# Attention and MLP on one core: the second batch's coarse head pairs go between its local groups, their E into unit 0's h buffers

## The chip, the cores and the metric

The kernel runs on 1 core of one Trainium2 chip. The metric is the time of one execution on the device in microseconds, median of 3 runs. Lower is better. Engines are called PE (TensorE), DVE (VectorE), ACT (ScalarE), POOL (GpSimd) and SP (SyncE, which here only issues DMAs).

## What is computed

Four batches of 576 positions and 512 features (8 heads of 64). Attention is the sum of two parts: a coarse one, on q, k and v averaged over groups of four positions (144 x 144 scores a head), and a local one, in which a position sees only its neighbours at a distance under 4. Then a Fourier mix with a residual, a normalisation, an MLP with a residual, and a gated output layer.

```python
q_d, k_d, v_d = (x.reshape(B, H, Sd, 4, D).mean(axis=3) for x in (q, k, v))
out = np.repeat(sm_attn(q_d, k_d, v_d), 4, axis=2) + local_attn(q, k, v)   # |i - j| < 4
x = out.transpose(0, 2, 1, 3).reshape(B, S, H * D)
u = x + np.real(np.fft.fft(np.fft.fft(x, axis=1), axis=2))
un = (u - u.mean(-1)) / np.sqrt(var + 1e-06)
x = u + np.maximum(un @ w_ch1, 0.0) @ w_ch2
gate = 1.0 / (1.0 + np.exp(-causal_conv5(x, conv_w)))
out = (gate * (x @ w_val)) @ w_out
```

All in float32; large products run as three float16 products (high by high, low by high, high by low).

## The kernel before

**Units.** The MLP runs over 12 units of 192 positions, three to a batch, numbered 0 to 11; unit 3 is the first of the second batch (b = 1). A unit is 8 groups of hidden features (`h_group`, L1116, tile `ph`) and 8 of the second product (`c_group`, L1132, tile `pc`); it needs its normalised input `uh`, `ul` from `ln` (L986 to L1051). Unit 0 alone runs in float32 (`steps32`, L1072): its hidden features lie in four `h32` tiles, three of them from the "acc" tag with three buffers (L1079), read by its `c_group` (L1098), two groups a tile. `moe2_steps` (L1166) is the output layer of a unit: taps of the convolution, `val` (L1235), `out` (L1251).

**The order of the work.** Every piece of work is a Python step with a weight. `put` and `spread` (L1345 to L1353) give each step a position on one axis, where n to n + 1 is unit n; before 0 lies the start (first batch, weights of the MLP). All steps are then called in order of position (L1408). From the instructions so recorded, with that order as priority, the framework's planner makes the fixed order of each engine's queue, by its own estimate of durations: an instruction of lower priority goes ahead where the other isn't ready or finds no buffer. `urgent` (L174) raises a step's priority by a number of instructions; the Fourier steps ("F") and `ln` ("N") are raised by 3000, the second batch's local and coarse steps aren't.

**Attention of a batch** (`attn_steps`, L423). `dense` (L487) is the local part, in three groups of windows: `scores(g)` (L522: matmuls into two banks `dS`, maximum, exponentials `dP`, sums, products) and `values(g)` (L580: transposes `dPT`, copies `PT`, matmuls `dO`, copies to X). `lowres` (L696) is the coarse part: a step for `base`, the squares of v for a scale (L680), and for each of four head pairs a step with score matmuls `sc` (L713), maxima `nm` (L720), exponentials `E` (L727) and their normalisation (POOL for b = 1, L736), and a step with transposes `eT` (L753), copies `ET`, matmuls `po` with the pooled v (L763) and the copy to `base` (L767). Then `base` is added to X (L786), the second half of X goes through DRAM to be mirrored (L795 to L802, L862), and the Fourier steps follow (L836 to L965).

**Positions of the second batch.** The local part, the four loads and sums of v (`pool_v4`, L643) and the sums of k stand in `P_D[1]` = 0.02 to 0.94; the coarse part and all that follows in `P_E[1]` = 0.96 to 1.85; `ln` of unit 3 at `P_L[1]` = 2.1.

**Buffers.** The tag "E" (three buffers) holds E, ET, PT, `ptv` (the partial sum of v) and later the Fourier tiles. `dS` and `sc`, with the Fourier sums, take turns on the two PSUM banks of tag "t"; `dPT`, `dO`, `eT`, `po`, `val` and `out` on the two of tag "s" (L35 to L39). v's pieces use the two buffers of "pr". The weights of the output layer come as `raw` tiles into the "k" and "v" buffers of the local v windows (L339).

**Loads.** All go through `load` (L183) on SP's queue. While `chain["on"]` holds (up to position `S_CH` = 0.9, L1364) each is ordered behind the one loaded before it; from then on the planner puts them in any order. SP issues in order: one that waits for its buffer holds the rest.

Of the kernel before, what the change touches and what calls it, by code (L numbers as in the profile page):

```python
# [9 lines left out]
F32 = mybir.dt.float32  # L10
# [3 lines left out]
AF = mybir.ActivationFunctionType  # L14
# [5 lines left out]
SD = S // 4  # L20
QC = SD // 2
# [20 lines left out]
NORM_V = ((1, 0), (1, 1))  # L42
LN_V = ((0, 0), (0, 2), (1, 0), (2, 0), (3, 0))
CHAIN = True
S_CH = 0.9
S_LD = (-12.14, -11.9)
S_L1 = -11.85
S_K = -11.75
# [12 lines left out]
N_WARM = (8, 5, 14, 2, 2, 2)  # L61
S_G1 = (-6.8, -6.7)
S_G2 = (0.2, 0.44)
P_D = {1: (0.02, 0.94), 2: (2.0, 3.2), 3: (4.4, 6.0)}
P_E = {1: (0.96, 1.85), 2: (3.3, 4.5), 3: (6.1, 7.4)}
P_L = {1: 2.1, 2: 4.9, 3: 8.5}
P_T0 = ((0.75, 0.93), (1.0, 1.3), (1.6, 2.0))
EN_G = (1,)
SUM_V = ()
# [59 lines left out]
def attn_moe_kernel(ctx, tc, q_t, k_t, v_t, w1, w2, w_val, conv_t, w_out, c_feat, c_seq, c_band, c_eye, out):  # L129
# [48 lines left out]
        else:  # L178
            f()

    chain = {"on": CHAIN, "last": None}

    def load(**kw):  # L183

        if chain["on"] and chain["last"] is not None:
            with tc.issue_after(chain["last"]):
                i = nc.sync.dma_start(**kw)
        else:
            i = nc.sync.dma_start(**kw)
        chain["last"] = i.ins  # L190
# [232 lines left out]
    def attn_steps(b):  # L423
# [63 lines left out]
        def dense(sp):  # L487
# [170 lines left out]
            if b == 0:  # L658
# [3 lines left out]
                lr = pools[2:] + [(0.1, lambda kc=kc: pooled_v0(vw, kc)) for kc in range(3)] + steps[:]  # L662
                steps[:] = low
            es = [{} for _ in GROUPS]
            if first:
                steps.extend([(1.3, lambda: scores(0, es[0])), (2.6, lambda: scores(1, es[1]))] + pools + lr[2:4])
                steps.extend([(2.6, lambda: scores(2, es[2])), lr.pop(4)] + lr[4:7])
                del lr[:7]
            for r in range(len(GROUPS) + 1):
                if r < len(GROUPS) and not first:  # L670
                    steps.append((1.3 * len(GROUPS[r]), lambda r=r: scores(r, es[r])))
                if r > 0:
                    steps.append((0.5 * len(GROUPS[r - 1]), lambda r=r: values(r - 1, es[r - 1])))
                if r > LR0:
                    for _ in range(5):
                        if lr:
                            steps.append(lr.pop(0))
            steps.extend(lr + v1)

            def squares():  # L680
                for g in range(len(GROUPS)):
                    A.activation(out=vw[g], in_=vw[g], func=AF.Square, accum_out=d["ssv"][:, g:g + 1])

            if not first:
                d["squares"] = squares


        def scale_x():
# [7 lines left out]
        def lowres():  # L696
# [6 lines left out]
            for a in range(H // 2):  # L703
                lr = {}

                def f(a=a, lr=lr):
# [3 lines left out]
                    for qc in range(2):  # L710
                        for par in range(2):
                            r = slice(par * 64, par * 64 + 64)
                            T.matmul(  # L713
                                out=pss[par][:, qc], lhsT=d["qkT"][r, 0, a, qc * QC:(qc + 1) * QC],
                                rhs=d["qkT"][r, 1, a, :], start=True, stop=True,
                            )
                    for par in range(2):
                        ps = pss[par]
                        nm = tiny.tile([QC, 2], F32, tag="nm", name="nm")
                        i = V.tensor_reduce(out=nm, in_=ps, axis=AX.X, op=ALU.max)  # L720
                        if b == 0:
                            gates.append(i.ins)
                        A.activation(out=nm, in_=nm, func=AF.Copy, scale=-SCALE / 16)
                        E = prp.tile([QC, 2, SD], F32, tag="E", name="E", bufs=3) if b else startup.tile([QC, 2, SD], F32, tag="E0", name="E0", bufs=4)
                        su = tiny.tile([QC, 2], F32, tag="lsu", name="lsu")
                        for qc in range(2):
                            A.activation(  # L727
                                out=E[:, qc], in_=ps[:, qc], func=AF.Exp, scale=SCALE / 16,
                                bias=nm[:, qc:qc + 1], accum_out=su[:, qc:qc + 1],
                            )  # L730
                        V.tensor_scalar(out=su, in0=su, scalar1=1e-9, scalar2=None, op0=ALU.add)
                        i = V.reciprocal(out=su, in_=su)
                        if b == 0 and a == H // 2 - 1 and par:
                            gates1.append(i.ins)
                        if b in EN_G:
                            mul(G, E, E, su.unsqueeze(2).to_broadcast([QC, 2, SD]))  # L736
                        else:
                            for qc in range(2):
                                A.activation(out=E[:, qc], in_=E[:, qc], func=AF.Copy, scale=su[:, qc:qc + 1])
                        lr[par] = E  # L740
# [35 lines left out]
        else:  # L776
            dense(None)
            d.setdefault("cuts", []).append(len(steps))
            lowres()
            n_chain = len(steps)  # L780

        @step(2.7)
# [562 lines left out]
    def put(pos, f):  # L1345
        events.append((pos, len(events), f))
# [14 lines left out]
    spread([(1.0, lambda i=i: sumsq_w(i, "w2", i == 8, i == 15)) for i in range(8, 16)], *S_G2)  # L1361
    put(S_G2[1], lambda: urgent(w2_scale, "S"))
    put(S_LW2, lambda: [load_w(i) for i in range(8, 11)])
    put(S_CH, lambda: chain.update(on=False))  # L1364
    for steps, p in ((st[0]["loads"], S_LD), (a0[:c0], S_T0), (a0[c0:c1], S_S0), (a0[c1:], S_F0)):
        spread(steps, *p)
    for r, f, p in ((W1_ORDER, w_in, S_W1), (W1_ORDER[:4], w_out_, S_C0), (W1_ORDER[4:], w_out_, S_C1), (range(8, 16), w_in2, S_W2)):
# [92 lines left out]
```

## Time and profile before

| | us |
|---|---|
| median of 3 runs (733.96 to 735.82) | 734.01 |
| the profiled execution | 733.22 |
| its span, first to last instruction | 731.4 |
| PE busy | 682.0 (93%) |
| DVE busy | 468.5 (64%) |
| ACT busy | 326.3 (45%) |
| POOL busy | 111.7 (15%) |
| mean granted clock of PE | 0.965 of full |

The profiler records one execution. A line is an instruction, or several alike, on one engine: line of the kernel, operation, written tile <- read tiles, shape. Times in a timeline are us from the start of the span. Idle time in brackets is that of the engine just before the instruction, with what ended it. Busy times of pipelined matmuls overlap, so the time of a row of several is not their sum. The granted clock is a share of full speed (1.00 is 2.4 GHz).

### The profile page before, as it was taken

The numbers are of one execution on the slowest core, as the hardware profiler recorded it, in microseconds if no ns is written. First come the engines' busy times: TensorE is split into PE (matmuls) and PEld (weight loads), VectorE is DVE, ScalarE is ACT, GpSimd is POOL, SyncE is SP. The second block draws the span as 40 slices with busy tenths as digits, with TensorE's granted clock in tenths as the row PEclk, the third lists the DMA queues.
The fourth block names the chain that finished last, engine by engine and source line by source line (L and its number), as shares of the span: only waits on it lengthen the run. The fifth ranks groups of instructions, "written<-read, shape, count | busy, mean of one in ns | idle before, by whom it ended". The sixth has DMA issues, their size and how long they took to land. (4 is left out here: it accounts for less than half of the span.)

```text
span 731.4 us, 18333 instructions
## 1 busy us (share of the span) xinstructions
PE 682.0 (93%) x7785; PEld 594.6 (81%) x7785; DVE 468.5 (64%) x983; ACT 326.3 (45%) x998; POOL 111.7 (15%) x158
## 2 busy tenths in 40 slices
PE   8488799997999877999999999999999999999997
PEld 4255598987899666868898898789899989999895
DVE  4888699997856597365976824829635572633324
ACT  2674273894433356756433825644413132222212
POOL 0400012124112121330203106003100010000000
PEclk9758999999999979999999999999999999999999
DMA  9965251524413100240230001003000000000001
GB/s 245 380 222 179 81 213 61 133 74 146 143 50 100 61 2 17 77 141 16 72 109 2 24 17 43 16 2 95 20 16 15 2 15 17 2 15 2 30 2 44
DMA packets 27574, 53.01 MB, mean 72 GB/s; under 512 B 2112, under 2 KB 16320, under 8 KB 26468
## 3 DMA queue, kind: packets, MB, share of 16 engines
q1 hardware_dynamic: 27492, 51.84, 22.1%
q8 instruction: 61, 1.00, 0.6%
q14 instruction: 21, 0.17, 0.1%
HBM read 45.34 MB, written 8.26 MB: 73 GB/s over the span
## 5 line engine op out<-in xcount | busy, mean ns | idle before, releaser
L1123 PE MATMUL ph<-uh,W 128*128 128x192 f16 x1408 | 195.2, 247 | 1.4 <-ACT uh L1049 1.4
L1123 PEld LDWEIGHTS <-W 128*128 128x128 f16 x2112 | 176.6, 98 | 9.2 <-issue 7.2
L1123 PE MATMUL ph<-ul,W 128*128 128x192 f16 x704 | 173.9, 247 | 2.5 <-DVE ul L1050 2.5
L1143 PE MATMUL pc<-hh,W 128*128 128x192 f16 x1232 | 171.4, 246 | 0.0
L1143 PEld LDWEIGHTS <-W 128*128 128x128 f16 x1848 | 152.8, 98 | 8.3 <-issue 7.1
L1143 PE MATMUL pc<-hl,W 128*128 128x192 f16 x616 | 150.9, 246 | 1.2 <-DVE hl L166 1.2
L166 DVE SCALAR_TENSOR_TENSOR hl<-ph,hh 128x384 f16<-128x384 f32 x88 | 48.4, 551 | 93.0 <-ACT hh L1127 92.6
L1127 ACT ACTIVATE hh<-ph 128x384 f16<-128x384 f32 x88 | 43.3, 492 | 102.9 <-PE ph L1123 99.9
L166 DVE SCALAR_TENSOR_TENSOR W<-X,cw,W 128x192 f32<-128x192 f32 x160 | 61.7, 440 | 1.2 <-ACT W L1198 1.0
L1235 PE MATMUL val<-yy,W 128*128 128x192 f16 x576 | 54.8, 251 | 0.0
L1235 PEld LDWEIGHTS <-W 128*128 128x128 f16 x576 | 49.6, 100 | 3.1 <-issue 1.0
L570 ACT ACTIVATE dP<-dS,dmx 128x64 f32<-128x64 f32 x160 | 47.9, 333 | 0.7 <-PE dPT L591 0.3
L1251 PE MATMUL out<-W,gh 128*128 128x512 f16 x144 | 45.6, 379 | 0.0
L570 ACT ACTIVATION_READ_ACCUMULATOR dP<-dS,dmx 128x1 f32 x160 | 36.3, 227 | 0.0
L166 DVE SCALAR_TENSOR_TENSOR W<-W,W 128x1024 int32<-128x1024 int32 x24 | 28.4, 1215 | 0.1
L1251 PE MATMUL out<-W,gl 128*128 128x512 f16 x72 | 27.3, 379 | 0.0
L727 ACT ACTIVATE E<-sc,nm 72x144 f32<-72x144 f32 x64 | 23.5, 376 | 6.7 <-PE po L763 3.7
L1143 PE MATMUL pc<-hh,Wz 128*128 128x192 f16 x176 | 25.1, 246 | 1.1 <-DVE X L172 1.1
L1143 PEld LDWEIGHTS <-Wz 128*128 128x128 f16 x264 | 22.0, 98 | 4.1 <-DVE X L172 1.4
L1251 PEld LDWEIGHTS <-gh 128*128 128x128 f16 x144 | 14.1, 98 | 13.7 <-issue 0.2
L1085 PE MATMUL ph<-u,W 128*128 128x192 f32 x128 | 24.2, 344 | 1.0 <-DVE u L1008 1.0
L1198 ACT ACTIVATE W<-X,cw 128x192 f32<-128x192 f32 x40 | 15.6, 451 | 20.9 <-DVE X L166 19.0
(246 smaller groups left out, 1203.0 us busy)
## 6 DMA issues: line engine op xcount, KB each, us to landing
W<-in_moe_w_ch_dram SPq DMA_DIRECT2D x12, 1024.0 KB
v<-in_v_dram SPq DMA_DIRECT2D x32, 144.0 KB
out_dram<-osb SPq DMA_DIRECT2D x17, 256.0 KB
vw<-in_v_dram SPq DMA_DIRECT2D x16, 256.0 KB
X<-in_q_dram SPq DMA_DIRECT2D x6, 576.0 KB
kT<-in_k_dram SPq DMA_DIRECT2D x4, 582.0 KB
X<-in_moe_w_ch_dram SPq DMA_DIRECT2D x2, 1024.0 KB
raw<-in_moe_w_ch_dram SPq DMA_DIRECT2D x4, 512.0 KB
```

The costliest lines, as they stand in the source:

```text
L166: return eng.scalar_tensor_tensor(out=out, in0=in0, scalar=scalar, in1=in1, op0=op0, op1=op1)
L570: A.activation(out=s_[:, z, a], in_=pss[par][:, z, a], func=AF.Exp, scale=SCALE, bias=mx[:, par, z, a:a + 1], accum_out=su[:, par, z, a:a ...
L727: A.activation(out=E[:, qc], in_=ps[:, qc], func=AF.Exp, scale=SCALE / 16, bias=nm[:, qc:qc + 1], accum_out=su[:, qc:qc + 1],)
L1085: i = T.matmul(out=ps[:, e], lhsT=W[AT[kc * 2 + m // 8] + 1][:, o:o + 128], rhs=u()[:, kc, :], start=(kc == 0), stop=(kc == 3))
L1123: T.matmul(out=ps[:, e], lhsT=w1_ap(pw, kc, 2 * g + e), rhs=uh[px][:, kc, :], start=(t == 0), stop=(t == 11))
L1127: A.activation(out=h_, in_=ps, func=AF.Relu)
L1143: T.matmul(out=ps[m // 2][:, m % 2], lhsT=w2_ap(pw, kk, m), rhs=x[px][:, e, :], start=(kk == 0 and (pw, px) == (0, 0) and m % 2 == 0), sto ...
L1198: A.activation(out=m, in_=x, func=AF.Copy, scale=w)
L1235: T.matmul(out=ps[:, e], lhsT=wv_ap(pw, kc, 2 * mh + e), rhs=m_["y"][px][:, kc, :], start=(t == 0), stop=(t == 11))
L1251: T.matmul(out=ps, lhsT=(gh, gl)[px][:, kc, t * 128:(t + 1) * 128], rhs=wo_ap(pw, kc), start=(n == 0), stop=(n == 11))
```

## The change

- The four head pairs of the second batch no longer stand behind its local part. `dense` itself calls `lowres` for b = 1 and mixes the steps: scores 0, scores 1, values 0, first half of pair 0, scores 2, values 1, second half of pair 0, first half of pair 1, values 2, and the rest of the pairs; the pieces of v stand between them from the start, the sums of k ahead of all.
- E of a pair is one tile [72, 2, 2, 144] of the tag "acc" for b = 1.
- `S_CH` is 1.3, so all of the second batch's loads are in the chain, and every later load is ordered behind the last of the chain.
- `P_D[1]` is 0.02 to 1.2 and holds local and coarse part; `P_E[1]` is 1.21 to 1.75 and holds what follows; `P_L[1]` is 1.9.

```diff
-S_CH = 0.9
+S_CH = 1.3
-P_D = {1: (0.02, 0.94), 2: (2.0, 3.2), 3: (4.4, 6.0)}
-P_E = {1: (0.96, 1.85), 2: (3.3, 4.5), 3: (6.1, 7.4)}
-P_L = {1: 2.1, 2: 4.9, 3: 8.5}
+P_D = {1: (0.02, 1.2), 2: (2.0, 3.2), 3: (4.4, 6.0)}
+P_E = {1: (1.21, 1.75), 2: (3.3, 4.5), 3: (6.1, 7.4)}
+P_L = {1: 1.9, 2: 4.9, 3: 8.5}
@@ load
+        elif chain["after"] is not None:
+            with tc.issue_after(chain["after"]):
+                i = nc.sync.dma_start(**kw)
@@ dense (squares is defined ahead of this)
+            if b == 1:
+                low = steps[:]
+                del steps[:]
+                lowres()
+                lr = steps[:]
+                steps[:] = low + v1[4:] + lr[:1]
+                cs = lr[2:]
+                sx = cs.pop(3)
+                sg = lambda g: (1.3 * len(GROUPS[g]), lambda: scores(g, es[g]))
+                og = lambda g: (0.5 * len(GROUPS[g]), lambda: values(g, es[g]))
+                steps.extend([sg(0), v1[0], sg(1), v1[1], og(0), cs[0], v1[2], sg(2), v1[3], og(1), cs[1], cs[2], og(2),
+                          cs[3], cs[4], (0.1, squares), sx, cs[5], cs[6], cs[7]])
+                return
@@ lowres
+                    Ep = acc_t("E", [QC, 2, 2, SD]) if b == 1 else None
...
-                        E = prp.tile([QC, 2, SD], F32, tag="E", name="E", bufs=3) if b else startup.tile([QC, 2, SD], F32, tag="E0", name="E0", bufs=4)
+                        E = Ep[:, par] if b == 1 else prp.tile([QC, 2, SD], F32, tag="E", name="E", bufs=3) if b else startup.tile([QC, 2, SD], F32, tag="E0", name="E0", bufs=4)
@@ attn_steps
-            lowres()
+            if b > 1:
+                lowres()
@@ the plan
-    put(S_CH, lambda: chain.update(on=False))
+    put(S_CH, lambda: chain.update(on=False, after=chain["last"]))
```

## Rows read from the trace of the kernel before

**Rows 1.** Busy time by stretch: bounds, length, five engines, granted PE clock, DMA.

```profile
90.00:252.00 162.00, 153.41 (x1691) 139.93 (x1691) 130.44 (x234) 86.25 (x244) 35.90 (x50) 0.99 0.36 111
140.00:200.00 60.00, 54.01 (x694) 48.07 (x692) 52.30 (x115) 39.29 (x116) 18.20 (x22) 1.00 0.39 119
252.00:279.60 27.60, 16.16 (x220) 13.65 (x218) 25.96 (x62) 15.24 (x50) 5.52 (x6) 0.80 0.01 2
258.27:268.51 10.24, 7.72 (x65) 6.45 (x66) 9.11 (x24) 7.15 (x26) 2.56 (x2) 0.50 0.01 2
278.75:282.16 3.41, 2.67 (x17) 2.52 (x17) 1.68 (x4) 3.41 (x25) 0.00 (x0) 0.50 0.00 0
```

**Rows 2.** Timeline of PE, 250 to 284: start, us, what, idle before.

```profile
258.85 0.59 PE L254 MATMUL tot<-ss_wo,ones 128*128 128x1 f32 x2 [4.86 <-DVE ss_wo L366]
...
263.51 0.98 PE L1002 MATMUL st<-sq,ones 128*128 128x192 f32 x2 [1.94 <-DVE sq L172]
...
279.49 0.32 PE L1123 MATMUL ph<-ul,W 128*128 128x192 f16 x1 [2.47 <-DVE ul L1050]
```

**Rows 3.** Timeline of DVE, 254 to 281.

```profile
278.49 0.95 DVE L1050 TENSOR_TENSOR ul<-uc,uh 128x768 f16<-128x768 f32 x1
```

**Rows 4.** Timeline of POOL, 138 to 218.

```profile
177.30 0.94 POOL L172 TENSOR_TENSOR vr<-vr,ptv 72x256 f32<-72x256 f32 x1
...
216.34 1.21 POOL L172 TENSOR_TENSOR X<-X,base 128x576 f32<-128x576 f32 x1 [5.47 <-ACT base L767]
```

**Rows 5.** Timeline of PE, 138 to 204: third local group's and coarse scores.

```profile
141.68 0.60 PE L538 MATMUL dS<-bandb 128*128 128x512 bf16 x2
...
154.88 0.89 PE L713 MATMUL sc<-qkT 64*72 64x144 f32 x8
...
171.58 0.71 PE L713 MATMUL sc<-qkT 64*72 64x144 f32 x4
...
190.44 0.89 PE L713 MATMUL sc<-qkT 64*72 64x144 f32 x8
...
198.62 0.71 PE L713 MATMUL sc<-qkT 64*72 64x144 f32 x4
```

**Rows 6.** Timeline of DVE, 138 to 218: maxima of the head pairs.

```profile
159.62 0.81 DVE L720 TENSOR_REDUCE nm<-sc 72x2 f32<-72x288 f32 x2
...
179.65 0.44 DVE L720 TENSOR_REDUCE nm<-sc 72x2 f32<-72x288 f32 x1
...
194.21 0.80 DVE L720 TENSOR_REDUCE nm<-sc 72x2 f32<-72x288 f32 x2
...
200.62 0.44 DVE L720 TENSOR_REDUCE nm<-sc 72x2 f32<-72x288 f32 x1
...
202.38 0.45 DVE L720 TENSOR_REDUCE nm<-sc 72x2 f32<-72x288 f32 x1
```

**Rows 7.** Timeline of ACT, 138 to 218: exponentials of the head pairs.

```profile
172.11 0.36 ACT L727 ACTIVATE E<-sc,nm 72x144 f32<-72x144 f32 x1
...
204.64 0.37 ACT L727 ACTIVATE E<-sc,nm 72x144 f32<-72x144 f32 x1
```

**Rows 8.** Timeline of SP's queue, 120 to 220: DMA issues.

```profile
162.60 0.36 SPq L189 DMA_DIRECT2D raw<-in_moe_w_val_dram  x1
163.06 0.34 SPq L187 DMA_DIRECT2D v<-in_v_dram  x1
```

**Rows 9.** Tile h: its readers; ns least, median, most, first and last start.

```profile
L1098 PE MATMUL pc<-h,W x128: 326/326/430, 118.1 to 154.6; 128*128 128x192 f32 x128
```

**Rows 10.** Third batch: timelines of DVE (405 to 413) and PE (446 to 452).

```profile
411.29 0.95 DVE L1050 TENSOR_TENSOR ul<-uc,uh 128x768 f16<-128x768 f32 x1
...
450.21 0.25 PE L1123 MATMUL ph<-uh,W 128*128 128x192 f16 x1
```

**Rows 11.** Timeline of POOL: the same addition at two places.

```profile
160.35 2.32 POOL L172 TENSOR_TENSOR ptv<-v 72x256 f32<-72x256 f32 x1
...
303.41 0.72 POOL L172 TENSOR_TENSOR ptv<-v 72x256 f32<-72x256 f32 x1
```

More of the change, by code (lines that the diff above doesn't have):

```diff
@@ L179, in urgent @@
             f()
-    chain = {"on": CHAIN, "last": None}
+    chain = {"on": CHAIN, "last": None, "after": None}
     def load(**kw):
@@ L664, in dense, with squares @@
             es = [{} for _ in GROUPS]
+            def squares():
+                for g in range(len(GROUPS)):
+                    A.activation(out=vw[g], in_=vw[g], func=AF.Square, accum_out=d["ssv"][:, g:g + 1])
+            if not first:
+                d["squares"] = squares
             if first:
@@ L678, in dense @@
             steps.extend(lr + v1)
[L680 to L685, printed above, removed]
         def scale_x():
```

## The prediction

> **What bounds the kernel now.** I read the busy time of the engines in a few stretches first, then TensorE's own timeline where it idles, then the chain of work behind that idle time. From 90 to 252 us TensorE is busy 153.4 of 162 us, at full clock; from 252 to 279.6 us it is busy only 16.2 of 27.6 us and the mean granted clock falls to 0.80 [rows 1]. So the kernel is bound by TensorE almost everywhere, and this hole is the largest loss behind the start. It costs 27.6 - 16.16 = 11.4 us of idleness. In two pieces in and just behind it the clock is granted at 0.5 (1.2 GHz, the lower of the two levels): 7.72 and 2.67 us of busy time there would take half as long at 2.4 GHz, so they lose 3.9 + 1.3 = 5.2 us. Together 16.6 us.
>
> The gaps say what the hole waits for. TensorE sits idle 4.86 us before 258.85, 1.94 us before 263.51 and 2.47 us before 279.49 [rows 2]. The last ends when `ul`, the low half of the second batch's first normalised unit, is written at 278.49 + 0.95 = 279.44 us [rows 3]: unit 3 can't begin without it. Ahead of `ul` stand that unit's normalisation and the batch's Fourier part, which began when the last coarse result had been added to X, at 216.34 + 1.21 = 217.55 us [rows 4]. From there to `ul` it takes 279.44 - 217.55 = 61.9 us. Unit 2 ends near 252 us, so the coarse part of the second batch comes about 27 us too late.
>
> Why is it late? The score matmuls of its four head pairs start at 154.88, 171.58, 190.44 and 198.62 us [rows 5]. The maxima of the first are taken at 159.62 us [rows 6], but its last E is written only at 172.11 us [rows 7]. In the first pair exponentials stand 11 us behind their maxima, in the last the first one stands at 204.64 us [rows 7], 3.6 us behind a maximum that ended at 200.62 + 0.44 us [rows 6]. They share three "E" buffers with PT, ET and the pooled v. And v itself is late: the fourth transfer is issued at 163.06 us, right behind a weight transfer at 162.60 that had blocked SP's queue [rows 8], so `vr` is whole only at 177.30 + 0.94 us [rows 4]. No pair can finish before.
>
> **The change, part by part.** *Positions.* From the steps' weights I worked out where each step is placed, in units of the main loop. The third group's scores move from 0.46 to 0.52, the last group's values from 0.79 to 0.90; the first head pair from 0.97 to 0.42, the second from 1.02 to 0.81, the third from 1.08 to 0.99, the fourth from 1.13 to 1.10. The addition to X stays (1.19 to 1.21). The positions alone thus promise nothing for the end; what they change is who gets a buffer first. The narrower range of the Fourier steps and the earlier normalisation cost and bring nothing by my count: those are marked urgent, so they run when their inputs are there.
>
> *E in another buffer.* The four pair tiles take the three buffers that unit 0's h had. The matmuls that read h run from 118.1 to 154.6 us [rows 9], the first buffer's in the first quarter of that, so the first pair finds its buffer free at 142 us, and the fourth takes the first pair's again. This removes the wait for "E".
>
> *The two score banks.* Local scores and head pairs take turns on two PSUM banks. Let H be the time for which a pair holds them. The third group's scores got them at 141.68 us and gave them up at 154.88 us [rows 5], which is 13.2 us. In the new order the first pair goes ahead of that group, the others behind it. So the fourth pair starts at 141.68 + H + 13.2 + 2H = 154.9 + 3H. In before it took 217.55 - 198.62 = 18.9 us from there to X, of which 3.2 us was the wait for "E" (3.6 less 0.4 for scaling the maximum): 15.7 us. So X is ready at **170.6 + 3H**. With the "E" wait taken out H is the time to the end of the second maximum plus 2.6 us (scaling, and four exponentials at 0.57 us): 160.43 - 154.88 + 2.6 = 8.1; 180.09 - 171.58 + 2.6 = 11.1; 195.01 - 190.44 + 2.6 = 7.2; 202.83 - 198.62 + 2.6 = 6.8 [rows 5 to 7]. The mean is 8.3; H lies between 6.8 and 11.1. As it stood in before, with the "E" wait, the first pair held them 172.66 - 154.88 = 17.8 us.
>
> With H = 8.3 X is ready at 195.5 us instead of 217.55, **22 us sooner** (26.5 at 6.8; 13.7 at 11.1).
>
> *v.* The eight transfers stay in the chain, so they go out one after another from 129 us on, ahead of the third batch's X and of the weights for the second layer. SP's queue holds these behind them; each waits for VectorE or GpSimd to free a buffer. `vr` should be whole near 160 us, before the first pair needs it. What is moved behind is covered: the third batch's unit starts at 450.21 us with its `ul` written at 411.29 + 0.95 us [rows 10], 38 us of slack; the weights are first used inside the hole. If that cover goes, each us that these weights come late is a us in which the hole can't be filled, up to the 4 us below. No DMA is added.
>
> *The squares* for the scale of the second batch move from 0.97 to 1.08: three ScalarE operations, still before the Fourier steps. I take nothing; the lower bound is nothing too, the upper about 2 us, the time in which those weights wait for the v buffers that the squares still read.
>
> *Crowding.* From 140 to 200 us VectorE is busy 52.3 of 60 us, ScalarE 39.3, and TensorE idles 6.0 us [rows 1]. The work of the first pairs moves into its first half, where weights are still being split. Nothing in before shows this mixture. I bound it from -2 us (part of the idle time there is the pairs' own and goes) to +6 us (it doubles) and take +2, nearer to the first since only two pairs move by much.
>
> *The sum.* `ul` comes at 279.4 - 22 = 257.4 us. Unit 2's end leaves 5.2 us of hole, in which the 1.1 us of weight squares and perhaps val matmuls fit; I leave 2 us idle (0 to 4). Of 16.6 us, 14.6 is won, less 2 for crowding: 12.6 us. The profiled execution took 733.2 us, of which the span is 731.4; 733.2 - 12.6 = 720.6. The median of the runs is 0.8 us higher, 734.0, so I predict **721 us**. With H = 6.8, no idle rest and -2 for crowding, 18.6 us are won: 715 us.
>
> A rule that speaks against the change stands in the Trainium skill, "SBUF — State Buffer", section "SBUF: two separate sides": a GpSimd instruction and a VectorE one with two SBUF inputs share a port pair as an exclusive lock, and the later one fully blocks; by it the sum comes out at the first rival's time, without it at the forecast's. The trace agrees on GpSimd's side: one addition of v took 2.32 us at 160.35 us, beside a busy VectorE, and 0.72 us at 303.41 us [rows 11].
>
> **The rivals.** *The hole is halved only (H of 11 or more).* Twelve additions of v and eight products of E on GpSimd, 0.7 us each, are pushed into the stretch where VectorE is 87% busy; if VectorE loses as much to each, it loses 20 x 0.7 = 14 us, 3.5 us for each of four pairs, so H = 11.8 and X is ready at 206 us, 11.5 us sooner. Then unit 3 starts near 268 us. Of the hole go the 2.47 us and about 1.5 of the 11.4 - 4.86 - 1.94 - 2.47 = 2.1 us of smaller gaps, and 1.3 + 0.3 us of slow clock: 5.6 us, less 2 for crowding, so 3.6 us: **730 us** (728 without crowding, 726 with -2). For it speaks the pair with 11.1 us; against it that the same twenty operations already ran between 137 and 211 us. The full block that the Trainium skill's page states is this case.
>
> *Slower: the pairs hold the banks as long as before.* If H stays at 17.8 us, because maxima queue on VectorE or ScalarE's exponentials queue behind the weights' splits, local groups stand behind the first pair and X is ready at 170.6 + 53.4 = 224 us, 6.5 us later than now. Then the hole grows by 6.5 us of idleness: 734 + 6.5 = **740 us**. It decides from H = 15.6 on, where X is no sooner than now. Against it: 11 of these 17.8 us were the wait for "E", which the change takes out.
>
> *It doesn't do what it says.* The order on the engines is a planner's; the last pair and the addition to X keep their positions (1.13 to 1.10, 1.19 to 1.21). If the planner only shuffles the pairs, or the hole is held by the weights of the second layer, **734 us**.
>
> **How the numbers follow.** The forecast (715 to 726): 0.58. Halved (726 to 732): 0.20. Nothing: 0.09. Slower: 0.13. About 0.3%, 2.2 us, is what a measurement of this kernel can tell from no change. So faster 0.77 (the halved hole's last 0.01 lies inside that), same 0.10, slower 0.13. The first two cases and the edge of the third hold 0.8: 715 to 733 us.
>
> **What would show it.** Right: the fourth pair's scores near 180 us and X added near 195; `vr` whole near 160; exponentials 1 us or less behind their maxima; `ul` of unit 3 near 257; in the stretch around 252 to 260 at most 4 us idle and no row of the clock at 0.5. Wrong: `sc` banks held over 11 us; TensorE idle well over 6 us from 140 to 200; the hole ending as now while X is early, which would put the bound in the Fourier or the normalising leg (61.9 us taken as unchanged), VectorE being 94% busy in the hole [rows 1].

## The result and the profile after

The changed kernel takes **741.13 us** (median of 4 runs, 738.56 to 741.33); the kernel before took 733.99 us beside it. The ratio is 1.0084, 95% interval 1.0056 to 1.0111: **slower by 7.1 us**, where 721 was forecast and 733 was the upper end. The profiled execution took 738.56 us, its span is 736.8 us. The text below names lines of the changed kernel; `sc` stands at L729 there, `E` at L744, `ul` at L1068.

Busy time by stretch of the kernel after, in the columns of [rows 1], answers that group:

```profile
90.00:252.00 162.00, 148.38 (x1619) 136.83 (x1620) 129.65 (x231) 84.75 (x242) 36.24 (x50) 0.97 0.35 109
140.00:200.00 60.00, 55.00 (x685) 49.33 (x683) 50.72 (x105) 39.12 (x119) 16.49 (x22) 0.97 0.27 86
252.00:282.30 30.30, 23.69 (x337) 18.98 (x338) 28.45 (x72) 20.35 (x73) 7.59 (x7) 0.89 0.04 11
275.85:286.09 10.24, 7.00 (x89) 5.62 (x85) 9.00 (x22) 8.30 (x39) 2.81 (x2) 0.50 0.05 14
228.06:231.47 3.41, 3.08 (x21) 2.96 (x22) 3.33 (x7) 1.43 (x3) 0.00 (x0) 0.50 0.19 59
166.63:170.04 3.41, 3.41 (x23) 2.89 (x22) 3.38 (x7) 3.41 (x6) 0.00 (x0) 0.50 0.02 5
```

The hole is still there. It is fuller than before (30.30 - 23.69 = 6.6 us idle instead of 11.4), but not by work won: the val matmuls stood in it before too (72 of them from 264.3 us, 72 from 263.3 us after). What is new in it is what TensorE didn't get done ahead of it. It has lost 5 us of busy time there (148.38 us up to 252 us instead of 153.41), and the last product of unit 2 (`pc`) ends at 264.1 us instead of 251.1. The hole ends 2.8 us later. Three pieces ahead of it, of which two are shown, and one at its end run at a granted clock of 0.50.

The timeline of TensorE after, scores of the first pair, of the third local group, of the second to fourth pairs, that group's transposes and values, the longest gap, and the last matmul of unit 2's `pc` (start, us, what, idle before):

```profile
136.07 0.71 PE L729 MATMUL sc<-qkT 64*72 64x144 f32 x4
140.73 0.46 PE L729 MATMUL sc<-qkT 64*72 64x144 f32 x2
151.31 0.38 PE L541 MATMUL dS<-bandb 128*128 128x512 bf16 x1
164.02 0.71 PE L729 MATMUL sc<-qkT 64*72 64x144 f32 x4 [2.03 <-ACT dP L573]
176.69 0.71 PE L729 MATMUL sc<-qkT 64*72 64x144 f32 x4
184.29 0.60 PE L594 MATMUL dPT<-eye,dP 128*128 128x128 f32 x4
187.57 0.68 PE L614 MATMUL dO<-PT,vw 64*64 64x58 f32 x16
194.65 0.71 PE L729 MATMUL sc<-qkT 64*72 64x144 f32 x4
228.39 0.67 PE L893 MATMUL ab<-feat,FH 128*97 128x128 f16 x4 [4.29 <-ACT FH L871]
263.81 0.25 PE L1161 MATMUL pc<-hh,W 128*128 128x192 f16 x1
```

Against [rows 5]: the third local group's scores start at 151.31 us instead of 141.68, and the fourth pair's at 194.65 instead of 198.62. VectorE's timeline has the two maxima of the first pair with a weight split between them, the wait behind the 4.29 us gap, and `ul`:

```profile
137.97 0.44 DVE L737 TENSOR_REDUCE nm<-sc 72x2 f32<-72x288 f32 x1
141.19 1.75 DVE L166 SCALAR_TENSOR_TENSOR W<-W,s_w 128x1024 f16<-128x1024 f32 x1
143.38 0.44 DVE L737 TENSOR_REDUCE nm<-sc 72x2 f32<-72x288 f32 x1
226.35 0.43 DVE L304 TENSOR_SCALAR W<-raw 128x512 int32<-128x512 int32 x1 [4.76 <-DMA raw<-in_moe_w_out_dram]
281.27 0.96 DVE L1068 TENSOR_TENSOR ul<-uc,uh 128x768 f16<-128x768 f32 x1
```

ScalarE's has a weight split that it waits for, the first exponential of the first pair and the last local copy to X:

```profile
142.98 1.15 ACT L380 ACTIVATE W<-W,s_w 128x1024 f16<-128x1024 f32 x1 [2.73 <-DVE W L166]
147.58 0.36 ACT L744 ACTIVATE E<-sc,nm 72x144 f32<-72x144 f32 x1
191.53 0.97 ACT L620 ACTIVATE X<-dO 128x456 f32<-128x456 f32 x2
```

GpSimd's has the last addition of v and the last addition of the coarse part to X, and answers [rows 4]:

```profile
150.76 0.73 POOL L172 TENSOR_TENSOR vr<-vr,ptv 72x256 f32<-72x256 f32 x1
210.74 1.21 POOL L172 TENSOR_TENSOR X<-X,base 128x576 f32<-128x576 f32 x1 [4.67 <-ACT base L784]
```

SP's queue: all eight v transfers, then the first and the last issue of the weights of the second layer (value and output weights), which answer [rows 8]:

```profile
129.81 17.27 SPq L187 DMA_DIRECT2D v<-in_v_dram  x8
170.36 9.77 SPq L190 DMA_DIRECT2D raw<-in_moe_w_val_dram  x2
...
217.80 3.28 SPq L190 DMA_DIRECT2D raw<-in_moe_w_out_dram  x1
```

So v did what was forecast and more (whole at 151.5 us; 178.2 before). The coarse part is ready at 210.74 + 1.21 = 211.95 us, only **5.6 us sooner, not 22**. From there to `ul` it takes 282.2 - 212.0 = **70.2 us, not 61.9**. The last weight transfer, issued at 196.2 us before, is issued at 217.80 us, 21.6 us later, and it stands in the chain of work that ended last (start, us, what), as the longest piece of 200 to 232 us:

```profile
217.80 8.53 DMA raw<-in_moe_w_out_dram
```

### The profile page after: what moved, and what is told of

Its sections match the earlier page's. It is cut to its first block, busy times and chain, and to the rows that moved or that the text cites. A ratio compares the mean times of both kernels' runs of the same rounds, so it can differ in the third digit from the quotient of the medians.

```text
span 736.8 us, 18316 instructions
## 1 busy us (share of the span) xinstructions
PE 684.5 (93%) x7785; PEld 597.5 (81%) x7785; DVE 467.0 (63%) x983; ACT 325.8 (44%) x998; POOL 115.1 (16%) x158
## 3 DMA queue, kind: packets, MB, share of 16 engines
q1 hardware_dynamic: 27492, 51.84, 21.7%
## 4 chain that ended last, share of the span: by engine, by line
PE 58%; DVE 23%; DMA 8%; ACT 7%; POOL 2%; issue 1%; SPq 1%; ACTq 0%; DVEq 0%; POOLq 0%
PE pc L1161 18%; PE ph L1141 16%; DVE W L166 9%; PE out L1269 5%; PE val L1253 5%; ACT dP L573 3%; DMA raw<-in_moe_w_out_dram 3%; DMA v<-in_v_dram 2%; DVE W L304 1%; PE po L780 1%; PE ab L893 1%; DVE X L172 1%; DMA X<-in_moe_w_ch_dram 1%; DVE qkT L625 1%; DVE dmx L562 1%
## 5 line engine op out<-in xcount | busy, mean ns | idle before, releaser
L1161 PEld LDWEIGHTS <-Wz 128*128 128x128 f16 x264 | 24.1, 104 | 4.7 <-issue 1.4
L1161 PE MATMUL pc<-hh,Wz 128*128 128x192 f16 x176 | 27.5, 261 | 0.0
L729 PE MATMUL sc<-qkT 64*72 64x144 f32 x128 | 20.7, 321 | 5.1 <-ACT dP L573 4.0
L744 ACT ACTIVATE E<-sc,nm 72x144 f32<-72x144 f32 x64 | 23.6, 382 | 3.6 <-PE po L780 2.4
L1269 PEld LDWEIGHTS <-gh 128*128 128x128 f16 x144 | 14.1, 98 | 13.5 <-issue 0.2
```

Of the source, the lines that this page charges most:

```text
L729: T.matmul(out=pss[par][:, qc], lhsT=d["qkT"][r, 0, a, qc * QC:(qc + 1) * QC], rhs=d["qkT"][r, 1, a, :], start=True, stop=True,)
L744: A.activation(out=E[:, qc], in_=ps[:, qc], func=AF.Exp, scale=SCALE / 16, bias=nm[:, qc:qc + 1], accum_out=su[:, qc:qc + 1],)
L1161: T.matmul(out=ps[m // 2][:, m % 2], lhsT=w2_ap(pw, kk, m), rhs=x[px][:, e, :], start=(kk == 0 and (pw, px) == (0, 0) and m % 2 == 0), sto ...
L1269: T.matmul(out=ps, lhsT=(gh, gl)[px][:, kc, t * 128:(t + 1) * 128], rhs=wo_ap(pw, kc), start=(n == 0), stop=(n == 11))
```

## Where the time is: what TensorE loses

Windows of the same five stretches, kernel before, kernel after, and the kernel **a_f0late** of the experiments below; the last line of each is the sum:

```profile
95.00:135.00 40.00, 38.82 (x361) 37.35 (x360) 38.19 (x53) 23.10 (x65) 6.92 (x13) 1.00 0.53 168
135.00:200.00 65.00, 59.01 (x748) 53.01 (x746) 56.34 (x121) 43.29 (x133) 19.73 (x23) 1.00 0.37 113
200.00:252.00 52.00, 51.63 (x575) 45.92 (x573) 31.27 (x56) 16.83 (x41) 9.24 (x15) 1.00 0.25 74
252.00:300.00 48.00, 36.49 (x526) 30.99 (x524) 38.11 (x90) 30.36 (x116) 8.41 (x9) 0.86 0.05 16
300.00:330.00 30.00, 27.29 (x315) 21.90 (x313) 14.55 (x46) 18.23 (x57) 13.15 (x18) 1.00 0.42 119
sum 235.00, PE 213.24 PEld 189.16 DVE 178.46 ACT 131.82 POOL 57.46; mean PE 42.65 PEld 37.83 DVE 35.69 ACT 26.36 POOL 11.49
```

```profile
95.00:135.00 40.00, 37.22 (x339) 35.65 (x338) 37.76 (x52) 22.26 (x66) 8.74 (x13) 0.96 0.51 165
135.00:200.00 65.00, 60.00 (x725) 53.88 (x724) 55.36 (x112) 43.80 (x139) 18.69 (x24) 0.97 0.27 85
200.00:252.00 52.00, 47.44 (x542) 43.86 (x540) 32.17 (x62) 15.88 (x36) 8.80 (x14) 0.97 0.34 106
252.00:300.00 48.00, 40.11 (x543) 32.12 (x541) 39.38 (x98) 31.80 (x122) 10.93 (x10) 0.89 0.07 22
300.00:330.00 30.00, 29.19 (x332) 24.51 (x332) 13.75 (x43) 17.48 (x52) 12.36 (x18) 0.95 0.42 119
sum 235.00, PE 213.95 PEld 190.02 DVE 178.42 ACT 131.22 POOL 59.53; mean PE 42.79 PEld 38.00 DVE 35.68 ACT 26.24 POOL 11.91
```

```profile
135.00:200.00 65.00, 63.29 (x777) 56.74 (x776) 56.85 (x126) 46.30 (x146) 23.29 (x26) 1.00 0.30 97
200.00:252.00 52.00, 49.45 (x574) 43.97 (x573) 38.66 (x74) 18.10 (x33) 10.38 (x15) 1.00 0.31 95
252.00:300.00 48.00, 44.39 (x679) 39.46 (x676) 32.29 (x75) 33.62 (x133) 13.29 (x15) 0.96 0.14 38
...
sum 235.00, PE 223.25 PEld 198.22 DVE 183.74 ACT 138.24 POOL 61.62; mean PE 44.65 PEld 39.65 DVE 36.75 ACT 27.65 POOL 12.32
```

A stretch less its busy time is idleness; half of the busy time in a piece with clock 0.50 (1.2 GHz, the lower of the two levels) is lost too, since it would take half as long at the other. Both were summed over every such gap and piece. From 95 to 330 us TensorE idles 21.8 us before and 235 - 213.95 = 21.1 us after: the same. But the pieces at 0.50 lose 5.2 us before and 10.2 us after (7.00, 3.08 and 3.41 us above and two more of 3.4 us, halved). The sum of both, made the same way for every kernel of this study (the experiments below), goes with the time of its profiled execution (the labels stand at the experiments; sums are of unrounded values):

| kernel | idle + slow clock, 95 to 330 us | profiled time | time less loss |
|---|---|---|---|
| before | 21.8 + 5.2 = 27.0 | 733.2 | 706.2 |
| after | 21.1 + 10.2 = 31.2 | 738.6 | 707.4 |
| b_ep | 21.7 + 5.1 = 26.8 | 735.1 | 708.3 |
| b_ep_v | 17.8 + 10.5 = 28.4 | 736.5 | 708.1 |
| b_epv_pos | 17.9 + 10.0 = 27.9 | 734.6 | 706.7 |
| a_free | 21.8 + 9.4 = 31.2 | 738.9 | 707.7 |
| a_w3 | 17.5 + 7.0 = 24.5 | 731.8 | 707.3 |
| a_sg2 | 14.1 + 4.4 = 18.5 | 727.2 | 708.7 |
| a_f0late | 11.8 + 3.3 = 15.1 | 721.2 | 706.1 |
| a_loc | 18.7 + 4.6 = 23.3 | 734.6 | 711.3 |
| fl_sq | 10.9 + 4.0 = 14.9 | 723.8 | 708.9 |
| fl_nov | 12.2 + 5.2 = 17.4 | 725.0 | 707.6 |
| fl_pos | 16.6 + 2.9 = 19.5 | 729.0 | 709.5 |
| b_warm | 13.7 + 4.7 = 18.4 | 733.0 | 714.6, of which 4.5 are its extra matmuls |

So the time is TensorE's work plus what it loses: what is left over lies between 706 and 711 us, while the loss runs from 14.9 to 31.2. For the idleness this is arithmetic. What the table tests is the clock: with the idleness alone taken off, the rest would run from 709 to 719 us. Each kernel has one profile, whose time can lie some us off its median (734.6 against 730.78 in a_loc, 729.0 against 732.61 in fl_pos). After has won 5.2 us of the hole (16.7 lost in 252 to 300 us before, 11.5 after) and lost 9.7 us ahead of it: 3.3 in 95 to 135 us, 0.7 in 135 to 200, 5.7 in 200 to 252. Less 0.3 behind the hole, that is the 4.2 us between the two sums. Of these the 3.3 us moves from kernel to kernel (a_f0late has 4.2 us there and is the fastest). What I put down to the change is the 5.7 us from 200 to 252 us, in the Fourier part: a_free below, which has the same wait there, loses 7.8 us in that stretch, and a_w3, which hasn't, 0.5.

## The experiments

**The parts alone (b_ep, b_ep_v).** Two kernels build the change up from before. The first, b_ep, only puts E into the buffers that h had:

```
-  E = prp.tile([QC, 2, SD], F32, tag="E", name="E", bufs=3) if b else ...
+  Ep = acc_t("E", [QC, 2, 2, SD]) if b == 1 else None      # once for both
+  E = Ep[:, par] if b == 1 else prp.tile(...)
```

> The kernel before, with one part of the change: E of the second batch's head pairs in one tile of the "acc" tag. Theory A (the wait for the three E buffers was real, and what went wrong in the change is its order, with the first pair ahead of the third local group): v is still late (whole near 178 us), but the pairs no longer queue for E, so base is added to X near 205 us instead of 217.6, the hole shrinks, 726 to 731 us. Rival B (the E buffers bound nothing, the order of the planner does): X near 217 as before, 733 to 735 us.

Measured: 735.32 us, ratio 1.0016 (0.9987 to 1.0045). X is ready at 211.9 us, 5.6 us sooner, and `ul` stays at 279.3.

The second, b_ep_v, also puts v's four steps among the first local steps:

```
   steps.append((1.3 * len(GROUPS[r]), lambda r=r: scores(r, es[r])))
+  if b == 1:
+      steps.extend(v1[:1] if r < 2 else v1[:2])
+      del v1[:1 if r < 2 else 2]
```

> The kernel before, with two parts of the change: E in "acc" tiles, and the four pieces of v between the local groups, so that their loads and sums come early; the head pairs stay behind the local part and the later loads stay free. Theory A: vr whole near 150 us, X ready near 197 us, 721 to 727 us, faster than before. Rival B: no faster than 733 us, X near 215.

Measured: 735.13 us, 0.9998 (0.9973 to 1.0023). `vr` is whole at 152.7 us, 25.6 us sooner, and X is ready at 212.9, `ul` at 280.5. Here TensorE idles 4.0 us less than before and loses 5.4 us more to the clock, most of it behind this gap:

```profile
161.49 2.56 PE L611 MATMUL dO<-PT,vw 64*64 64x58 f32 x64 [5.05 <-ACT PT L597]
```

Neither the "E" wait nor v sets the end: in both kernels X gains 5 us and the leg from X to `ul` loses 5.5 (67.4 and 67.6 us). What lengthens that leg shows below, at the places of the Fourier steps.

**The order of the later loads (a_free).** Are the weights late because the change ties all later loads into one sequence? One edit, from after:

```
-  put(S_CH, lambda: chain.update(on=False, after=chain["last"]))
+  put(S_CH, lambda: chain.update(on=False))
```

> The changed kernel without the last edge: loads after the chain are free of it, as in before. Theory A (the output layer's weights are late because the local v windows whose buffers they take are read late): first weight load within 3 us of 170 and the last near 220 as in the changed kernel, 739 to 742 us. Rival C (they are late because they are ordered behind v's transfers): the weights are issued from about 163 us, the last before 205, VectorE's wait of 4.8 us in the Fourier part is gone, 733 to 737 us.

Measured: 739.64 us, 1.0066 (1.0041 to 1.0092); the weight transfers go out at 169.1 to 217.5 us, as late as in after. So their order isn't what holds them. By the program they take the buffers of the local groups' k and v windows, which the group's values and the squares free; the last local copy to X ends at 192.5 us in after, 22.8 us later than before (169.7).

**The first pair's place (a_f0late).** From after, the first pair's scores move behind the second group's values, and its second step and the second pair's scores behind the third's (`cs` holds scores and second step of each pair in turn):

```
-  ... og(0), cs[0], v1[2], sg(2), v1[3], og(1), cs[1], cs[2], og(2), cs[3], ...
+  ... og(0), v1[2], sg(2), v1[3], og(1), cs[0], og(2), cs[1], cs[2], cs[3], ...
```

> The changed kernel with the first head pair moved behind the third local group's scores and the second group's values, nothing else. Theory A: the third group's scores start near 142 us instead of 151 to 154, the last local copy to X is back near 170 instead of 191, the weights of the output layer are in before 205, 725 to 733 us. Rival C (the load order) and rival D (the narrower placing of all that follows): 738 us or more, the copies still near 190.

Measured: **723.46 us** (721.17 to 724.45), 0.9833 (0.9800 to 0.9866): 17.7 us faster than after, 10.7 faster than the kernel before, which took 734.20 us beside it. The third group's scores stand at 140.07 us again, its last copy to X ends at 169.8, the last weight transfer leaves at 199.6:

```profile
140.07 0.39 PE L541 MATMUL dS<-bandb 128*128 128x512 bf16 x1
...
182.01 0.71 PE L729 MATMUL sc<-qkT 64*72 64x144 f32 x4
```

```profile
204.66 1.21 POOL L172 TENSOR_TENSOR X<-X,base 128x576 f32<-128x576 f32 x1 [9.19 <-ACT base L784]
```

```profile
267.73 0.94 DVE L1068 TENSOR_TENSOR ul<-uc,uh 128x768 f16<-128x768 f32 x1
```

X is 11.7 us sooner than before, `ul` 10.8, the end 10.7: nearly one for one. So in this order of the steps the forecast's link from X to the end holds, at half of the gain in X that it had.

**How much of it is one exchange (a_sg2)?** From after, only the third group's scores change places with the first pair; it still stands ahead of both remaining value steps:

```
-  ... og(0), cs[0], v1[2], sg(2), v1[3], og(1), ...
+  ... og(0), sg(2), cs[0], v1[2], v1[3], og(1), ...
```

> The changed kernel with one exchange: the scores of the third local group go ahead of the first coarse head pair, which still stands ahead of both remaining value steps. Theory A (the two score banks are the cause: the first pair's scores hold them from 136 to 149 us, and the third group's scores wait behind them): the third group's scores come at 140 to 143 us again (after: 151.3), its last copy to X at 169 to 173 (after: 192.5), the output layer's weights start with them, and the time is 722 to 729. Rival B (it is the amount of pair work that stands ahead of the values, on TensorE and ScalarE, not the banks): scores at 141 but the last copy to X stays at 185 to 192, and the time is 735 to 741.

Measured: 726.75 us, 0.9879 (0.9819 to 0.9938), in theory A's range. But only its first sign came: the scores start at 139.8 us, while the last copy to X ends at 189.8 and the last weight transfer leaves at 211.3, as rival B has it. Neither theory was right as a whole. The end doesn't hang on the copy; what is better is VectorE's longest wait for a weight transfer in the Fourier part (2.3 us instead of 4.8, 2.3 in all instead of 7.3), and TensorE's loss from 135 to 252 us (3.5 us instead of 12.8).

**All local groups first (a_loc).** From after, four pairs behind all local groups, the squares right behind those; the scores of a pair also go ahead of the second step of the pair before it:

```
+  ... sg(2), v1[3], og(1), og(2), (0.1, squares), cs[0], cs[2], cs[1], sx, cs[4], cs[3], ...
```

> The changed kernel with all three local groups ahead of every coarse pair, the squares right behind them, and then the four pairs. Theory A (the local part's end sets the window buffers, the weights and VectorE's queue): the last copy to X at 166 to 170 us, the eighth weight transfer of the output layer at 185 to 195 (217.8 after, 199.6 with the first pair moved behind one group's values), the base added at 206 to 213, time 720 to 728. Rival B (the pairs' own chain sets the end: four pairs in the two banks behind 165 us): the base is added at 213 to 220 and the time is 729 to 736.

Measured: 730.78 us, 0.9937 (0.9902 to 0.9972). The local part ends at 171.9 us and X is ready at 209.7, within A's range, but the last weight transfer leaves at 205.6, not 195, and the time is in B's. So local work first isn't the rule: it is 7.3 us behind a_f0late, in which the first pair runs beside the third group. How much of that is the pairs' own new order isn't shown.

**The squares' place and v's place, in the fast order (fl_sq, fl_nov).** From a_f0late, the squares right behind the third group's values:

```
-  ... og(2), cs[1], cs[2], cs[3], cs[4], (0.1, squares), sx, ...
+  ... og(2), (0.1, squares), cs[1], cs[2], cs[3], cs[4], sx, ...
```

> The kernel that took 723.46 us (first pair behind the second group's values) with the squares of the v windows moved from behind the third pair to right behind the third group's values. Theory A (the weights still wait for the window buffers that the squares read): the fourth to eighth transfers start 8 to 13 us sooner (184 to 200 us as it stands) and the time is 718 to 722. Rival B (with the hole nearly filled TensorE's work sets the end and the weights are no longer late): the transfers start sooner but the time is 722 to 725.

Measured: 724.07 us, 0.9840 (0.9791 to 0.9889), and the transfers don't even go sooner (185.5 to 200.6). Nothing, as the prediction took the squares.

From a_f0late, v's four steps behind the third group's values:

```
+  ... og(1), cs[0], og(2), v1[0], v1[1], v1[2], v1[3], cs[1], ...
```

> The same 723.46 us kernel with the four v steps behind the third group's values, so that v is whole only behind the local part as in the kernel before (178 us instead of 151). Theory A (the pairs need v ahead of 175 to gain): the first base copy slips from 175.3 to 181 to 188 us, the base is added at 211 to 216 instead of 205.9, and the time is 728 to 734. Rival B (the first pair's values aren't on the path, only the third group's place is): 722 to 726.

Measured: 724.32 us, 0.9843 (0.9790 to 0.9896). `vr` is whole at 177.7 us as before and X ready at 210.4, 4.5 us later than in a_f0late, yet `ul` comes only 2.3 us later and the time isn't measurably longer: rival B. The early v isn't what the gain needs.

**The places of the Fourier steps (fl_pos, b_epv_pos).** From a_f0late, back to the places of before:

```
-  P_E = {1: (1.21, 1.75), ...};  P_L = {1: 1.9, ...}
+  P_E = {1: (1.21, 1.85), ...};  P_L = {1: 2.1, ...}
```

> The 723.46 us kernel (the changed one with the first pair behind the second group's values) with the Fourier steps and the norm at the places that they had before the change (ends 1.85 and 2.1 instead of 1.75 and 1.9 units). Theory A (the earlier base can only be used if the steps behind it stand sooner too): base added at 205 to 208 as it stands, but `ul` at 275 to 280 instead of 268.7, and 729 to 734 us. Rival B (the order on the engines follows from readiness, the places don't bind): `ul` at 267 to 270 and 722 to 725 us.

Measured: 732.61 us, 0.9970 (0.9944 to 0.9996): theory A, 9 us for two numbers, though `ul` comes at 274.0 us, just below its range. X is ready at the same 205.9 us, but VectorE's timeline has a piece of the weights' scaling between the halves of the Fourier part's end:

```profile
235.08 0.75 DVE L172 TENSOR_TENSOR X<-X,DS 128x289 f32<-128x289 f32 x1 [0.64 <-ACT DS L980]
240.93 0.69 DVE L410 TENSOR_REDUCE cvmx<-cv 128x1 f32<-128x512 f32 x1 [5.10 <-PE cv L408]
...
246.51 0.94 DVE L166 SCALAR_TENSOR_TENSOR DS<-pp,ivx,qs 128x289 f32<-128x289 f32 x2
```

VectorE takes its work in the order in which it stands, waits 5.10 us for a sum of squares of weights that the batch's chain doesn't need, converts weights, and only then ends the Fourier part, 7.4 us later than in a_f0late (249.2 against 241.8). The same wait stood in b_ep (4.26 us) and b_ep_v (5.10 us), whose legs are as long as the one here (68.1 us), and in the kernel before, unseen by the prediction (there VectorE then waited another 0.41 us for ScalarE's `qs`, which the Fourier part itself needs, so the wait held it up less):

```profile
250.18 0.69 DVE L407 TENSOR_REDUCE cvmx<-cv 128x1 f32<-128x512 f32 x1 [5.05 <-PE cv L405]
```

The places alone don't do it either. From b_ep_v with the sooner places:

```
+  P_E = {1: (0.96, 1.75), ...};  P_L = {1: 1.9, ...}
```

> The kernel before with the pairs' E in the accumulators, v's transfers early, and the Fourier steps and the norm at the sooner places of the change (1.75 and 1.9), but the old order of local groups and pairs; without the sooner places this was 735.13 us. Theory A (places bind): `ul` moves from 280.5 to 270 to 275 and the time is 725 to 730. Rival B (places don't bind, and without the new order the base stays at 213): `ul` 279 to 281, 733 to 736 us.

Measured: 733.59 us, 0.9981 (0.9956 to 1.0006). Here `ul` comes at 275.6, 4.9 us sooner, nearly as A says, and the time stays where B has it: 11.4 us are lost in 135 to 200 us, nearly half of it by the clock.

**VectorE's wait for the weights (a_w3).** From after, the words of the last two pieces (the conversion `W<-raw` of what was loaded) are taken behind the Fourier part's AL steps (the low half of its first product), and the range in which all steps of these weights stand begins later:

```
-  to_f32(W[i + 1]..., raw)
+  to_f32(W[i + 1]..., raw, lambda: st[1]["ALlast"].ins if i == 19 else None)
-  S_W3 = (1.35, 1.95)
+  S_W3 = (1.5, 1.95)
```

> The changed kernel with one exchange on VectorE: the words of the last two pieces of the output layer's weights are taken behind the Fourier part's AL steps, not between its first steps, where VectorE stood 4.8 us for a transfer. Theory A (the late weights cost the end what VectorE's wait costs): the 4.3 us gap of TensorE at 224 us goes, X's Fourier part is done at 249 to 251 (after 254.3), and the time is 735 to 738 (after 741.1). Rival B (the weights come later by as much and the norm behind them is held instead, or the end is set by what was lost ahead of 200 us): 739.5 to 742.

Measured: **731.86 us**, 0.9967 (0.9943 to 0.9991), better than A: 9.3 us faster than after with the local part as late as there (191.6 us) and X ready at 212.3. The Fourier part ends at 247.1 us instead of 254.3, `ul` at 276.4 instead of 282.2, the gap at 224 us is gone, and TensorE loses 0.5 us in 200 to 252 us instead of 6.1. VectorE takes the two pieces without a wait:

```profile
232.02 0.75 DVE L304 TENSOR_SCALAR W<-raw 128x512 int32<-128x512 int32 x2
```

So about half of the 17.7 us between after and a_f0late is this wait and what hangs on it. In the rest X is 6.4 us sooner in a_f0late. The run makes two changes, the two pieces and the range; which is worth how much wasn't separated.

**The price of the clock (b_warm).** From before, 20 matmuls that nothing reads, ahead of the 4.86 us gap of [rows 2]:

```
   def wo_scale():
+      ps = pst("po", [P, 512])
+      for _ in range(20):
+          with tc.issue_after(gram["last"].ins):
+              T.matmul(out=ps, lhsT=busy[:, 0:P], rhs=busy, start=True, stop=True)
```

> The kernel before with 20 matmuls of a constant tile (128x512, nothing reads them) ahead of the matmul that TensorE waits 4.86 us for at 254 us, so that TensorE works through that gap. Nothing else is changed; the order of some neighbours may shift. Theory A (the 5.2 us that TensorE loses at half clock in 252 to 279.6 us come from the gap and cost the end as much as idle time): the granted clock of 258 to 268 us is 1.0 instead of 0.5, and the time falls by 3 to 5 us to 729 to 731. Rival B (in the hole TensorE has work to spare, so that its clock there costs nothing): the clock rises, the time stays within 733 to 735. If the dummies run longer than the gap, slower: 735 to 738.

Measured: 734.93 us, 1.0013 (0.9986 to 1.0040). The gap is filled, the clock isn't mended: it falls 3.5 us later, in the next gap (2.32 us, where there were 1.94). Timeline of TensorE, and the window:

```profile
253.81 4.48 PE L416 MATMUL po<-busy 128*128 128x512 f16 x20
...
262.72 0.98 PE L1006 MATMUL st<-sq,ones 128*128 128x192 f32 x2 [2.32 <-DVE sof L166]
```

```profile
261.80:268.60 6.80, 5.88 (x34) 5.46 (x35) 6.40 (x14) 6.77 (x28) 2.45 (x2) 0.50 0.00 0
```

The end stays, by B's number but not for its reason: neighbours moved too (`ul` came at 275.9, 3.5 us sooner), and TensorE idles 8.2 us from 330 us to the end, where before it was 5.8. What the clock costs by itself is left open here; that it counts like idleness rests on the table above.

## Why the prediction was wrong, point by point

*The bound* was read rightly: where the hole closes, as in a_f0late, the time falls by what TensorE no longer loses (11.9 us of 27.0; the profiled time fell by 12.0, the median by 10.7).

*E in another buffer* took its wait away, and v came early, as said. Neither was what the end hung on (b_ep, b_ep_v, fl_nov). Whether a_f0late would need E in the accumulators wasn't tried.

*The two score banks* is the first step that failed, in two terms. H of the first pair was costed at 8.3 us, from pairs that ran behind the local part. It held the banks from 136.07 to 149.1 us, 13 us, without any wait for "E". The second half of its scores started 4.7 us behind the first (140.73 us); ScalarE read the other bank for a local group until 138.7. Its second maximum stands at 143.38 us behind local normalising and weight splits on VectorE, its exponentials at 147.58 behind ScalarE's share of the same, for which ScalarE also sat idle 2.73 us while the first maximum lay ready. That is the slower rival's mechanism. (The four exponentials themselves took 1.5 us, not 4 x 0.57.) The others took 11.0, 5.4 and 6.7 us. With these and the third group's 15 us (151.3 to 166.3) the banks were free for the fourth pair at 182.1 us. That this is near the 179.8 forecast is luck: the first pair started 5.6 us sooner than the sum has it, which made up for its length. But the fourth pair's scores started at 194.65, and that is the second term and the larger: TensorE's own order. TensorE wasn't idle; the group's late transposes (184.29) and values stand ahead of them. Why the transposes stand there, with `dP` normalised at 168.5 us, isn't shown. Of the 16.4 us by which X missed the forecast, 2.3 come from the banks, 12.5 from this order, and 1.6 from the way from the fourth pair to X (17.3 us instead of 15.7). The sum took the wait for a bank as the only thing that orders the pairs, though the prediction had found that the last pair's position hardly moves (1.13 to 1.10) and that "positions alone thus promise nothing". The rival that followed from that (it doesn't do what it says) had the place of X nearly right and was given 0.09.

*"What is moved behind is covered"* failed for the weights of the second layer. Their buffers are the local windows, so they follow the local part, which the first pair put off by 22.8 us. The prediction saw SP's queue and, under the squares, up to 2 us for the v buffers, and priced lateness at up to 4 us of unfilled hole. The price came elsewhere: VectorE's order holds the weights' words among the Fourier steps, so that the batch's own chain waited (a_w3: 9.3 us for moving these words).

*The 61.9 us leg taken as unchanged* was its other side: 70.2 us after, but 60.6 to 64.1 in the seven kernels that have the new places and wait for no weight transfer longer than 2.3 us there (a_f0late, a_sg2, a_loc, fl_sq, fl_nov, a_w3, b_epv_pos). The sentence that the sooner Fourier steps "cost and bring nothing by my count" missed 9 us (fl_pos): "they run when their inputs are there" isn't so behind a waiting instruction in the same queue. The text's last line had named this leg and VectorE's 94% as where it could be wrong, but gave it no price and no case.

*Squares and crowding.* The squares cost nothing by themselves (fl_sq). Crowding was taken at +2 us; from 140 to 200 us TensorE idles 5.0 us instead of 6.0, and 1.7 us go to the clock: inside the bounds.

*The halved rival and GpSimd.* The last addition of v took 0.73 us at 150.76 us, not the 2.32 of [rows 11], but VectorE did lose time beside them: the weight split at 141.19 us took 1.75 us (1.27 at 132.09 us, with no GpSimd work beside it), and the addition beside it, at 141.82, 1.72. Of VectorE's instructions from 135 to 157 us, those that ran beside an addition of v took 3.3 us more in all than the median of the same instructions with GpSimd idle; before, from 135 to 200 us, it was 1.8. That is the rival's mechanism at a quarter of the 14 us that it took. The 3.3 us lie where the first pair holds the banks; how much of its 13 us they are isn't shown. The section "SBUF: two separate sides" of the Trainium skill's page "SBUF — State Buffer" states a lock by which the later of the two blocks; these rows agree with it (one addition ran to 141.85 us when the split began, and the next ended 0.6 us behind the split).

*The slower rival* named 740 us, and 741 came. Its first half was right (banks held long by the first pair, local groups behind it), its second wasn't: X was 5.6 us sooner than before, not 6.5 later. The loss is in the leg behind X, so that its number came true is luck.

## What to carry to other kernels

When work is moved ahead of other work, list what is put off on every queue, the buffers which that work would have freed, the loads that wait for those buffers, and the instructions in some engine's order that wait for those loads; the price is paid where the last of these stands, not where the work was moved. A leg of a chain may be carried over unchanged only if nothing in its engines' order waits for something foreign to it: look in it for an idle time ended by a DMA or by another engine's side job (here 4.76 us and 5.05 us on VectorE). Then compare idle time and slow clock of the bounding engine by stretch, since a hole that gets fuller can be paid for ahead of it.

## What the runs showed of the hardware

The granted clock of TensorE fell to 0.50 behind gaps much shorter than the 4.86 us of [rows 2]: in the kernel after, behind one of 2.03 us and one of 0.81 us close together (the piece at 166.63 us above), in b_warm behind one of 2.32 us. Equal idleness thus cost 5 us more by the clock (21.1 us idle and 10.2 by the clock, against 21.8 and 5.2). Yet not every gap did so: a_f0late has one of 1.85 us at 208.9 us and runs at 1.00 throughout 200 to 252 us, and the kernel before has one of 2.02 us at 179.2 us and runs at 1.00 throughout 140 to 200 us. So the length of a single gap didn't tell whether the clock would fall.

A weight transfer took 8.53 us in the chain at 217.80 us, where the ones before it took 3.3 to 4.3 us in the same chain; its issue on SP lasted 3.28 us instead of 0.33. It went out right behind the Fourier part's transfers through DRAM (214.95 us). Whether these are the reason wasn't tried.
